# Weight loads issued by GpSimd, its copies and weight arithmetic moved to ScalarE and VectorE

## The chip, the cores and the metric

The kernel runs on one core of a Trainium2 chip. The time is the device time of one execution in microseconds (us); lower is better. The core has TensorE (PE, matmuls and transposes, results into PSUM), VectorE (DVE), ScalarE (ACT), GpSimd (POOL) and SyncE (SP), each with its own queue that it works off in order, and 16 DMA engines that all queues share.

## What is computed

Block-sparse attention over 4 batches, 8 heads, 768 positions in 24 blocks of 32, head size 64 (a block of queries sees its neighbours, the first and the last block and 3 sampled blocks; the first and the last block see all), and then a feed-forward layer (512 to 2048 to 512) with a rational activation on its output, 3072 tokens. Cut to what matters:

```python
def _attn_ref(q, k, v, sampled_blocks):
    scores = scale * np.matmul(q, k.transpose(0, 1, 3, 2))
    ...
    scores = np.where(mask, scores, -1000000000.0)
    attn = np.exp(scores - np.max(scores, axis=-1, keepdims=True))
    attn = attn / (np.sum(attn, axis=-1, keepdims=True) + 1e-09)
    return np.matmul(attn, v).astype(np.float32)

def _moe_ref(x, w_in, w_out, a, b):
    h = x @ w_in
    P = a[0] + a[1] * h + a[2] * h**2 + a[3] * h**3
    Q = 1.0 + np.abs(b[0]) * np.abs(h) + np.abs(b[1]) * h**2
    return ((P / (Q + 1e-06)) @ w_out).astype(np.float32)
```

All inputs arrive as 64-bit numbers (doubles and 64-bit integers). The kernel has to turn them into 32-bit floats itself where they are weights.

## The kernel before

The work is cut into small operations (`Op`), each with the engine or engines that may do it, a price in ns, what it must come after, and a priority (line 116). A planner, `issue` (line 162), goes through them at build time: it always takes the operation that can start first by its prices, ties by priority, and emits it. So the order of every queue is fixed before the run. Where an operation may go to several engines (`among`, line 140; the keys in `ALT = "copsk"` are open to all that are priced, others to the first alone), the planner takes another engine than the home one when the home would start over some 500 ns later (ScalarE 534, GpSimd 243). Operations over 8 priority units ahead of the current feed-forward unit wait. Loads on SyncE are planned on 8 lanes; loads on another queue are not.

*Weights* (`weights`, line 392). `w_in` and `w_out` come as 64-bit words in 16 + 16 pieces of 128 rows x 512 words (512 KB). `one` (line 405) makes for each piece: a load into one of two buffers `wl` (lines 413, 416), issued by SyncE, all in one chain (`behind`); a conversion from the upper words (`convert`, ScalarE, or GpSimd or VectorE); `pack1` to `pack3` on VectorE (lines 425, 428, 431; the last one frees the buffer). A piece of `w_out` is then split into a high part (`out_high`: ScalarE, GpSimd or VectorE) and a low part (`out_low`, line 442: home GpSimd, VectorE allowed). Pieces of `w_in` wait until the four of a group are there; ScalarE takes their largest values (line 375), and after a scale has been worked out (`w_scaled`, line 466) each is scaled (`scaled`, home GpSimd), rounded (`high`, ScalarE) and its rest taken (`low`, line 489, GpSimd).

*Attention* (`attention`, line 688) runs block by block: scores on TensorE (line 761), maxima on VectorE (line 771), exponentials on ScalarE (line 786), transposes on TensorE (line 828) and their eviction by ScalarE (`times`, line 148), values on TensorE (line 863). For batch 0 all keys lie in SBUF (`kall`). Before the scores of a block, GpSimd copies its three sampled key blocks (`copies`, lines 713 to 716; first it loads their numbers into registers, line 667) into one of two buffers `kx`, which the scores of the block two before must have released. Once, GpSimd also copies the first and the last key block (`edges`, line 916), before all `copies`. Later batches read keys by DMA. Values are gathered by DMA on SyncE's queue (lines 839 to 847), queries too (line 639).

*Feed-forward* (`unit`, line 942): 12 chunks of 256 tokens x 8 units. A unit is 24 matmuls (lines 959 to 961), three evaluations of their result on ScalarE (lines 966, 970, 980), and then lines 973 to 1004 on VectorE and two on ScalarE, and 12 matmuls into the output (lines 1015 to 1017). Units of the first two chunks wait for their pieces of the weights. The first units stand between blocks of attention; until the first of them, TensorE fills gaps with dummy matmuls (`fill`, line 160).

Of the kernel before, what the change touches and what calls it, by code (L numbers as in the profile page):

```python
# [11 lines left out]
F32 = mybir.dt.float32  # L12
# [11 lines left out]
def kernel(  # L24
# [367 lines left out]
    def weights():  # L392
# [12 lines left out]
        def one(prio, kind, u, x, before):  # L405
            d = {}
            s_wl = Slot(r_wl)
            s_w = Slot(r_dw) if kind else None

            def load():  # L410
                d["ld"] = early.tile([P, 2 * WC], I32, name="wl", bufs=2)
                if kind:
                    nc.sync.dma_start(out=d["ld"], in_=wo64[x * P:(x + 1) * P])
                    return
                r0 = head(x, 0) * D
                nc.sync.dma_start(out=d["ld"], in_=wi64[r0:r0 + P, u * 2 * WC:(u + 1) * 2 * WC])

            def convert(eng):
                d["w"] = early.tile([P, WC], I32, name="dw", bufs=3) if kind else wi[:, x, u].rearrange("p a n -> p (a n)").bitcast(I32)
                d["words"] = d["ld"].rearrange("p (n w) -> p n w", w=2)  # L420
                times(eng, d["w"].bitcast(F32), d["words"][:, :, 1].bitcast(F32), 2.0 ** -112)

            def pack1():
                w = d["w"]
                nc.vector.tensor_scalar(out=w, in0=w, scalar1=3, scalar2=None, op0=ALU.logical_shift_left)

            def pack2():
                nc.vector.scalar_tensor_tensor(out=d["w"], in0=d["words"][:, :, 0], scalar=29, in1=d["w"], op0=ALU.logical_shift_right, op1=ALU.bitwise_or)

            def pack3():  # L430
                nc.vector.scalar_tensor_tensor(out=d["w"], in0=d["words"][:, :, 1], scalar=-2 ** 31, in1=d["w"], op0=ALU.bitwise_and, op1=ALU.bitwise_or)

            def most():
                if u not in sums:
                    sums[u] = early.tile([P, 8], F32, name="sums")
                bound(d["w"].bitcast(F32), sums[u][:, x:x + 1])

            def out_high(eng):
                times(eng, wo_h[:, x], d["w"].bitcast(F32), 1.0)

            def out_low(eng):
                eng.tensor_tensor(out=wo_l[:, x], in0=d["w"].bitcast(F32), in1=wo_h[:, x].bitcast(F32), op=ALU.subtract)  # L442

            o0 = Op(SY, [(475, 524288)], load, (), prio - 2, takes=[s_wl], behind=before)
            w = [s_w] if kind else []
            o = Op(among("c", SC, sc=520, po=588, ve=335), 0, convert, [o0], prio, takes=w, uses=[s_wl])
            o = Op(VE, 335, pack1, [o], prio, uses=w)
            o = Op(VE, 602, pack2, [o], prio, uses=[s_wl] + w)
            o = Op(VE, 602, pack3, [o], prio, uses=[s_wl] + w)
            if kind:  # L450
                o1 = Op(among("o", SC, sc=520, po=588, ve=335), 0, out_high, [o], prio, uses=w)
                o2 = Op(among("p", PO, po=1225, ve=602), 0, out_low, [o1], prio, uses=w)
                out_ready[x] = [o2]
                decoded.append(o2)
                return o0, o2
            return o0, Op(SC, 613, most, [o], prio)
# [9 lines left out]
    def w_scaled(u, prio, group, sums):  # L466
# [10 lines left out]
        for x in range(NCC):  # L477
            def three(x):
                d, s_ws = {}, Slot(r_dw)

                def scaled(eng):
                    d["w"] = early.tile([P, WC], I32, name="dw", bufs=3).bitcast(F32)
                    times(eng, d["w"], wi[:, x, u].rearrange("p a n -> p (a n)").bitcast(F32), sc[0])

                def high(eng):
                    times(eng, wi[:, x, u, 0], d["w"], 1.0)

                def low(eng):
                    eng.tensor_tensor(out=wi[:, x, u, 1], in0=d["w"], in1=wi[:, x, u, 0], op=ALU.subtract)  # L489

                a = Op(among("s", PO, po=671, ve=396, sc=613), 0, scaled, [o], prio, takes=[s_ws])
                a = Op(among("h", SC, sc=520, po=588, ve=335), 0, high, [a], prio, uses=[s_ws])
                a = Op(among("l", PO, po=1113, ve=602), 0, low, [a], prio, uses=[s_ws])
                in_ready.setdefault(u, []).append(a)
                decoded.append(a)
            three(x)
# [191 lines left out]
    def attention(b, j, prio):  # L688
# [10 lines left out]
        for m, x in enumerate(xs):  # L699
            def one(m, x):  # L700
# [9 lines left out]
                elif near:  # L710
                    s_kx = Slot(r_kx)

                    def copies():
                        rows = sampled_rows(x, mybir.EngineType.Pool)
                        for r in range(NR):
                            nc.gpsimd.tensor_copy(out=kxs[:, s_kx.buf, r].rearrange("p h r -> p (h r)"), in_=kall[:, bass.ds(rows[r], 1)].rearrange("p o h r -> p (o h r)"))

                    a = Op(PO, 1500, copies, [o_setup, chain["edges"]], p - 1, takes=[s_kx], uses=s_kall)
                    deps.append(a)
                    kslots = [s_kx] + s_kall  # L720
                else:
# [443 lines left out]
```

## Time and profile before

| what | value |
|---|---|
| time, median of 3 runs | 870.55 us (868.5, 870.55, 905.55) |
| the profiled execution | 869.87 us |
| its span, first to last instruction | 868.1 us |
| PE busy | 812.3 us (94%) |
| DVE busy | 699.2 us (81%) |
| ACT busy | 578.8 us (67%) |
| POOL busy | 98.7 us (11%) |
| DMA issued through SyncE's queue | 135.27 MB, 60.2% of the 16 engines' span |

The span is what the profile covers; the execution's own time is 1.8 us longer. The busy times are for the whole span; the rows further down give them by stretch. A view by line gives, for a group of like instructions, how many there were, their busy time, the mean duration of one, and how long their engine stood idle just before them and for what. Register loads, branches and DMA issues are not counted as busy. Matmul ends are modelled, so a busy PE is not PE at its peak.

### The profile page before, as it was taken

The page shows a single profiled execution, that of the slowest core. Times are in us where ns is not written, and L with a number is a line of the kernel's source. Part 1 is how long each engine was busy: PE and PEld are TensorE (multiplying, and loading weights), DVE is VectorE, ACT ScalarE, POOL GpSimd, SP SyncE. Part 2 cuts the span into 40 slices and gives each one's busy share as a digit, 9 for nine tenths or more (in the row PEclk, how much of TensorE's full clock was granted, in tenths as well). Part 3 has the DMA queues.
Part 4 walks back from the last instruction along what each step waited for, and adds up shares of the span by engine and source line. Part 5 has one row for each costly group of instructions (what it writes and reads, how often), then busy time and mean ns, then how long its engine had stood idle before and what let it go on. Part 6 is the DMA issues. An engine that isn't in the chain of part 4 may idle for free.

```text
span 868.1 us, 26226 instructions
## 1 busy us (share of the span) xinstructions
PE 812.3 (94%) x10056; PEld 617.4 (71%) x10056; DVE 699.2 (81%) x1773; ACT 578.8 (67%) x1263; POOL 98.7 (11%) x139
## 2 busy tenths in 40 slices
PE   6897757987899999999999999999999999999997
PEld 3555545765677787777777777777777777778885
DVE  2666898999998887778888876877888878887885
ACT  4557477766576676876667677777666676667563
POOL 1332656453200000000000000000000000000000
PEclk9999977999999999999999999999999999999999
DMA  9779668438667866876658667775545646630000
GB/s 218 170 193 237 199 213 217 136 106 219 158 154 178 212 169 169 207 191 175 152 130 201 186 167 174 211 185 163 152 126 153 165 120 171 157 101 23 1 25 25
DMA packets 255916, 136.94 MB, mean 158 GB/s; under 512 B 63408, under 2 KB 245552, under 8 KB 255792
## 3 DMA queue, kind: packets, MB, share of 16 engines
q1 hardware_dynamic: 255792, 135.27, 60.2%
q8 instruction: 80, 1.31, 0.7%
q14 instruction: 44, 0.36, 0.2%
HBM read 124.20 MB, written 11.01 MB: 156 GB/s over the span
## 4 chain that ended last, share of the span: by engine, by line
PE 72%; DVE 12%; DMA 8%; SPq 4%; ACT 2%; issue 2%; ACTq 0%; DVEq 0%
PE acc L1015 9%; PE ph L959 9%; PE acc L1017 9%; PE acc L1016 9%; PE ph L960 8%; PE ph L961 8%; PE av L863 6%; PE m L761 6%; PE m L828 5%; DMA wl<-in_moe_w_out_dram 2%; PE m L522 2%; DMA ld<-in_k_dram 2%; DMA wl<-in_moe_w_in_dram 2%; DMA ld<-in_v_dram 1%; DMA ldq<-in_q_dram 1%
## 5 line engine op out<-in xcount | busy, mean ns | idle before, releaser
L959 PE MATMUL ph<-xh,wi 128*128 128x256 f16 x768 | 210.5, 274 | 1.1 <-DVE tt L976 1.1
L961 PE MATMUL ph<-xh,wi 128*128 128x256 f16 x768 | 209.4, 273 | 1.9 <-POOL wi L489 1.9
L960 PE MATMUL ph<-xl,wi 128*128 128x256 f16 x768 | 209.3, 273 | 0.9 <-DVE xl L908 0.9
L1015 PE MATMUL acc<-wo_h,gh 128*128 128x512 f32 x384 | 162.5, 423 | 0.6 <-ACT ld L148 0.5
L1017 PE MATMUL acc<-wo_h,gl 128*128 128x512 f32 x384 | 153.6, 400 | 7.9 <-DVE gl L1004 7.9
L1016 PE MATMUL acc<-wo_l,gh 128*128 128x512 f32 x384 | 152.7, 398 | 1.2 <-POOL wo_l L442 1.2
L966 ACT ACTIVATE sq<-ph,fc 128x512 f32<-128x512 f32 x96 | 65.9, 686 | 116.1 <-PE ph L961 115.6
L786 ACT ACTIVATE pr<-pr,st 128x256 f32<-128x256 f32 x224 | 111.3, 500 | 33.5 <-DVE st L797 33.4
L959 PEld LDWEIGHTS <-wi 128*128 128x128 f16 x768 | 75.2, 98 | 43.0 <-issue 24.0
L983 DVE SCALAR_TENSOR_TENSOR ab<-sq,absb,ab 128x512 f32<-128x512 f32 x96 | 73.0, 760 | 40.6 <-ACT ab L980 40.4
L771 DVE CUSTOM_DVE_ANT_1 pr<-m,bias 128x256 f32<-128x256 f32 x224 | 85.6, 419 | 12.9 <-PE m L761 12.3
L1017 PEld LDWEIGHTS acc<-wo_h,gl 128*128 128x128 f32 x384 | 72.8, 190 | 27.8 <-DVE gl L1004 10.7
L1015 PEld LDWEIGHTS acc<-wo_h,gh 128*128 128x128 f32 x384 | 73.1, 190 | 20.9 <-issue 6.3
L994 DVE SCALAR_TENSOR_TENSOR gh<-tt,par,rr 128x512 fp32r<-128x512 f32 x96 | 74.0, 771 | 15.8 <-PE acc L1016 8.4
L148 ACT ACTIVATE pT<-m 128x512 f32<-128x512 f32 x112 | 65.9, 594 | 29.3 <-PE m L828 28.7
L961 PEld LDWEIGHTS <-wi 128*128 128x128 f16 x768 | 75.1, 98 | 12.2 <-POOL wi L489 2.5
L1016 PEld LDWEIGHTS acc<-wo_l,gh 128*128 128x128 f32 x384 | 73.0, 190 | 14.5 <-POOL wo_l L442 2.1
L828 PEld LDWEIGHTS m<-ident,pr 128*128 128x128 f32 x448 | 67.8, 206 | 20.8 <-ACT pr L786 7.1
L828 PE MATMUL m<-ident,pr 128*128 128x128 f32 x448 | 75.3, 292 | 7.7 <-ACT pr L786 3.3
L960 PEld LDWEIGHTS <-wi 128*128 128x128 f16 x768 | 75.2, 98 | 7.8 <-issue 0.4
L863 PEld LDWEIGHTS av<-vg,pT 128*32 128x32 f32 x3584 | 55.8, 111 | 28.7 <-issue 13.7
L863 PE MATMUL av<-vg,pT 128*32 128x64 f32 x3584 | 72.4, 224 | 3.7 <-DMA vg<-in_v_dram 2.8
(114 smaller groups left out, 1338.5 us busy)
## 6 DMA issues: line engine op xcount, KB each, us to landing
vg<-in_v_dram SPq DMA_DIRECT2D x312, 64.0 KB, 3.2
vg<-in_v_dram SPq DMA_DIRECT2D x88, 192.0 KB, 3.6
vg<-in_v_dram SPq DMA_DIRECT2D x24, 512.0 KB, 4.6
kall<-ks SPq DMA_DIRECT2D x49, 192.0 KB, 2.8
kall<-ks SPq DMA_DIRECT2D x147, 64.0 KB, 2.1
wl<-in_moe_w_in_dram SPq DMA_DIRECT2D x16, 512.0 KB, 4.5
wl<-in_moe_w_out_dram SPq DMA_DIRECT2D x16, 512.0 KB, 3.9
kall<-ks SPq DMA_DIRECT2D x15, 512.0 KB, 5.2
```

Of the source, the lines that this page charges most:

```text
L771: nc.vector.tensor_tensor_reduce(out=prs[x][:, g].rearrange("p (s r) -> p s r", r=BLK), in0=h["sp"][g], in1=add.rearrange("p (s o) -> p s ...
L786: nc.scalar.activation(out=prs[x][:, g], in_=prs[x][:, g], func=AF.Exp, scale=SCALE, bias=st[:, 6 + g:7 + g], accum_out=st[:, 8 + 2 * m + ...
L828: nc.tensor.transpose(pp[:, jj * P:(jj + 1) * P], pr[:, g, kt:NS * BLK:2], ident)
L863: nc.tensor.matmul(av[rows, g], pT[:, 2 * g + kt, rows], vf[:, head(h4, g), kt * D:(kt + 1) * D], start=(kt == 0 and (n == 1 or (m == 0 an ...
L959: nc.tensor.matmul(o, wh, xh[:, :, cc], start=(cc == 0), stop=False)
L960: nc.tensor.matmul(o, wh, xl[:, :, cc], start=False, stop=False)
L961: nc.tensor.matmul(o, wl, xh[:, :, cc], start=False, stop=(cc == NCC - 1))
L983: nc.vector.scalar_tensor_tensor(out=d["ab"], in0=d["sq"], scalar=absb[:, 1:2], in1=d["ab"], op0=ALU.mult, op1=ALU.add)
L994: nc.vector.scalar_tensor_tensor(out=d["gh"], in0=d["tt"], scalar=par[:, 0:1], in1=d["rr"], op0=ALU.add, op1=ALU.mult)
L1015: nc.tensor.matmul(acc[:, t], ghs, wo_h[:, f], start=(new and e == 0), stop=False)
L1016: nc.tensor.matmul(acc[:, t], ghs, wo_l[:, f], start=False, stop=False)
L1017: nc.tensor.matmul(acc[:, t], gls, wo_h[:, f], start=False, stop=(last and e == 1))
```

## The change

Five things change, all in the first part of the run:

- the loads of weight pieces are issued by GpSimd instead of SyncE (planned at 1000 ns each);
- `convert` and `out_high` may go to ScalarE or VectorE, no longer to GpSimd;
- `out_low` and `low` go to VectorE;
- `scaled` has its home on ScalarE, and may go to VectorE;
- the copies of sampled key blocks, with the register loads before them, go to ScalarE.

GpSimd keeps `edges` and the few operations at the start.

```diff
-                    nc.sync.dma_start(out=d["ld"], in_=wo64[x * P:(x + 1) * P])
+                    nc.gpsimd.dma_start(out=d["ld"], in_=wo64[x * P:(x + 1) * P])
...
-                nc.sync.dma_start(out=d["ld"], in_=wi64[r0:r0 + P, u * 2 * WC:(u + 1) * 2 * WC])
+                nc.gpsimd.dma_start(out=d["ld"], in_=wi64[r0:r0 + P, u * 2 * WC:(u + 1) * 2 * WC])
...
-            def out_low(eng):
-                eng.tensor_tensor(out=wo_l[:, x], in0=d["w"].bitcast(F32), in1=wo_h[:, x].bitcast(F32), op=ALU.subtract)
-
-            o0 = Op(SY, [(475, 524288)], load, (), prio - 2, takes=[s_wl], behind=before)
+            def out_low():
+                nc.vector.tensor_tensor(out=wo_l[:, x], in0=d["w"].bitcast(F32), in1=wo_h[:, x].bitcast(F32), op=ALU.subtract)
+
+            o0 = Op(PO, [(1000, 524288)], load, (), prio - 2, takes=[s_wl], behind=before)
             w = [s_w] if kind else []
-            o = Op(among("c", SC, sc=520, po=588, ve=335), 0, convert, [o0], prio, takes=w, uses=[s_wl])
+            o = Op(among("c", SC, sc=520, ve=335), 0, convert, [o0], prio, takes=w, uses=[s_wl])
...
             if kind:
-                o1 = Op(among("o", SC, sc=520, po=588, ve=335), 0, out_high, [o], prio, uses=w)
-                o2 = Op(among("p", PO, po=1225, ve=602), 0, out_low, [o1], prio, uses=w)
+                o1 = Op(among("o", SC, sc=520, ve=335), 0, out_high, [o], prio, uses=w)
+                o2 = Op(VE, 602, out_low, [o1], prio, uses=w)
...
-                def low(eng):
-                    eng.tensor_tensor(out=wi[:, x, u, 1], in0=d["w"], in1=wi[:, x, u, 0], op=ALU.subtract)
-
-                a = Op(among("s", PO, po=671, ve=396, sc=613), 0, scaled, [o], prio, takes=[s_ws])
+                def low():
+                    nc.vector.tensor_tensor(out=wi[:, x, u, 1], in0=d["w"], in1=wi[:, x, u, 0], op=ALU.subtract)
+
+                a = Op(among("s", SC, sc=613, ve=396), 0, scaled, [o], prio, takes=[s_ws])
                 a = Op(among("h", SC, sc=520, po=588, ve=335), 0, high, [a], prio, uses=[s_ws])
-                a = Op(among("l", PO, po=1113, ve=602), 0, low, [a], prio, uses=[s_ws])
+                a = Op(VE, 602, low, [a], prio, uses=[s_ws])
...
-                        rows = sampled_rows(x, mybir.EngineType.Pool)
+                        rows = sampled_rows(x, mybir.EngineType.Activation)
                         for r in range(NR):
-                            nc.gpsimd.tensor_copy(out=kxs[:, s_kx.buf, r].rearrange("p h r -> p (h r)"), in_=kall[:, bass.ds(rows[r], 1)].rearrange("p o h r -> p (o h r)"))
-
-                    a = Op(PO, 1500, copies, [o_setup, chain["edges"]], p - 1, takes=[s_kx], uses=s_kall)
+                            nc.scalar.activation(out=kxs[:, s_kx.buf, r].rearrange("p h r -> p (h r)"), in_=kall[:, bass.ds(rows[r], 1)].rearrange("p o h r -> p (o h r)"), func=AF.Copy)
+
+                    a = Op(SC, 1100, copies, [o_setup, chain["edges"]], p - 1, takes=[s_kx], uses=s_kall)
```

## Rows read from the trace of the kernel before

**Rows 1.** The windows view: busy time of each engine (and number of instructions) in three stretches of the span, the granted TensorE clock as a share of full speed, the mean busy share of the 16 DMA engines, and GB/s.

```profile
0.00:80.00 80.00, 64.26 (x1013) 40.05 (x1013) 42.53 (x174) 46.80 (x123) 20.52 (x58) 0.96 0.88 209
80.00:240.00 160.00, 126.82 (x1648) 91.00 (x1648) 152.00 (x347) 106.15 (x233) 78.15 (x82) 0.93 0.66 177
240.00:868.10 628.10, 621.25 (x7398) 486.37 (x7396) 504.70 (x1253) 425.82 (x908) 0.00 (x0) 1.00 0.56 146
```

**Rows 2.** The lines view with shapes kept apart, VectorE (DVE), the stretch 0 to 240 us; columns: line, engine, operation, output<-inputs by tile, shapes, count | busy us, mean ns of one | idle before and what ended it.

```profile
L428 DVE SCALAR_TENSOR_TENSOR wi<-wl,wi 128x512 int32<-128x512 int32 x16 | 13.5, 842 | 0.1
L973 DVE TENSOR_TENSOR tt<-tt,sq 128x512 f32<-128x512 f32 x14 | 13.2, 941 | 0.0
L431 DVE SCALAR_TENSOR_TENSOR wi<-wl,wi 128x512 int32<-128x512 int32 x16 | 12.9, 808 | 0.1
L997 DVE SCALAR_TENSOR_TENSOR ab<-ab,gh 128x512 f32<-128x512 f32 x13 | 12.5, 959 | 0.0
L428 DVE SCALAR_TENSOR_TENSOR dw<-wl,dw 128x512 int32<-128x512 int32 x16 | 12.4, 776 | 0.1
L431 DVE SCALAR_TENSOR_TENSOR dw<-wl,dw 128x512 int32<-128x512 int32 x16 | 12.2, 760 | 0.0
L994 DVE SCALAR_TENSOR_TENSOR gh<-tt,par,rr 128x512 fp32r<-128x512 f32 x13 | 12.0, 919 | 0.0
L425 DVE TENSOR_SCALAR dw<-dw 128x512 int32<-128x512 int32 x16 | 11.6, 723 | 4.6 <-ACT dw L148 4.1 <-POOL dw L152 0.5
L983 DVE SCALAR_TENSOR_TENSOR ab<-sq,absb,ab 128x512 f32<-128x512 f32 x14 | 11.5, 821 | 3.7 <-ACT ab L980 3.7
L1000 DVE SCALAR_TENSOR_TENSOR tt<-tt,par,ab 128x512 f32<-128x512 f32 x13 | 11.5, 881 | 0.0
L1004 DVE TENSOR_TENSOR gl<-tt,rr 128x512 fp32r<-128x512 f32 x13 | 10.6, 816 | 0.0
L976 DVE SCALAR_TENSOR_TENSOR tt<-ph,fc,tt 128x512 f32<-128x512 f32 x13 | 9.6, 740 | 0.0
...
L425 DVE TENSOR_SCALAR wi<-wi 128x512 int32<-128x512 int32 x16 | 6.9, 432 | 8.6 <-ACT wi L148 4.9 <-POOL wi L152 3.7
```

**Rows 3.** The same view of VectorE, the stretch 240 to 868 us, in which GpSimd is idle.

```profile
L994 DVE SCALAR_TENSOR_TENSOR gh<-tt,par,rr 128x512 fp32r<-128x512 f32 x83 | 62.1, 748 | 15.8 <-PE acc L1016 8.4 <-ACT sq L966 4.4 <-PE acc L1017 2.6
...
L976 DVE SCALAR_TENSOR_TENSOR tt<-ph,fc,tt 128x512 f32<-128x512 f32 x83 | 61.9, 745 | 0.4
...
L1004 DVE TENSOR_TENSOR gl<-tt,rr 128x512 fp32r<-128x512 f32 x84 | 57.7, 687 | 2.0
L997 DVE SCALAR_TENSOR_TENSOR ab<-ab,gh 128x512 f32<-128x512 f32 x83 | 56.9, 685 | 0.0
```

**Rows 4.** The lines view of GpSimd (POOL), the whole span.

```profile
L716 POOL COPY kx<-kall 128x128 f32 x66 | 24.2, 404 | 37.8 <-PE m L761 34.3 <-issue 1.6 <-POOL kx L716 1.0
L442 POOL TENSOR_TENSOR wo_l<-dw,wo_h 128x512 fp32r<-128x512 f32 x16 | 23.3, 1458 | 20.5 <-ACT wo_h L148 20.0
L489 POOL TENSOR_TENSOR wi<-dw,wi 128x512 f16<-128x512 f32 x16 | 22.0, 1385 | 8.1 <-ACT wi L148 8.1
L152 POOL TENSOR_SCALAR dw<-wi,scw 128x512 f32<-128x512 f32 x13 | 11.6, 898 | 7.9 <-DVE scw L353 7.7
L152 POOL TENSOR_SCALAR wo_h<-dw 128x512 fp32r<-128x512 f32 x7 | 6.9, 984 | 19.6 <-DVE dw L431 14.0 <-DVE st L808 3.0 <-DVE st L811 2.7
L152 POOL TENSOR_SCALAR dw<-wl 128x512 f32<-128x512 f32 x6 | 5.3, 875 | 5.7 <-DMA wl<-in_moe_w_out_dram 5.7
L152 POOL TENSOR_SCALAR wi<-wl 128x512 f32<-128x512 f32 x6 | 4.4, 739 | 18.9 <-DMA wl<-in_moe_w_in_dram 18.9
```

**Rows 5.** The lines view with shapes kept apart, ScalarE (ACT), 0 to 240 us.

```profile
L786 ACT ACTIVATE pr<-pr,st 128x256 f32<-128x256 f32 x62 | 30.8, 499 | 12.9 <-DVE st L797 12.9
...
L148 ACT ACTIVATE wi<-wl 128x512 f32<-128x512 f32 x10 | 6.7, 673 | 11.1 <-DMA wl<-in_moe_w_in_dram 11.1
...
L148 ACT ACTIVATE wo_h<-dw 128x512 fp32r<-128x512 f32 x9 | 5.7, 630 | 9.2 <-DVE dw L431 9.2
...
L148 ACT ACTIVATE dw<-wi,scw 128x512 f32<-128x512 f32 x3 | 2.2, 719 | 0.9 <-POOL wi L489 0.9
...
L298 ACT ACTIVATE absb<-par 128x2 f32<-128x2 f32 x1 | 0.2, 203 | 3.4 <-DMA par<-in_moe_b_dram 3.4
```

**Rows 6.** The source view of line 667, the loads of a sampled block's number into a register: queue, operation, count: duration in ns as min/median/max, first and last start in us.

```profile
L667 POOLq TENSOR_LOAD <-ix x22: 726/730/2653, 17.2 to 170.5; - x22
```

**Rows 7.** The timeline of SyncE's queue: start us, duration us, line, transfer, how many in a row. The first three loads of weights.

```profile
13.33 0.43 SPq L416 DMA_DIRECT2D wl<-in_moe_w_in_dram  x1
...
29.32 1.85 SPq L416 DMA_DIRECT2D wl<-in_moe_w_in_dram  x2
```

**Rows 8.** The waits view of SyncE's queue, 0 to 240 us: who waited for whom, us in total, times, longest.

```profile
SPq L413 <- DVE dw L431: 17.5, 6, 7.3
```

**Rows 9.** The waits view of TensorE (PE), 0 to 240 us.

```profile
PE acc L1017 <- DVE gl L1004: 7.1, 5, 3.1
...
PE m L761 <- ACT kt L148: 3.3, 1, 3.3
PE m L828 <- ACT pr L786: 3.3, 3, 2.1
...
PE av L863 <- DMA vg<-in_v_dram: 2.8, 3, 1.5
```

## What the change is predicted to do

> **What bounds the kernel now.** Read the windows view first. After 240 us TensorE is busy 621.25 of 628.10 us at the full clock and GpSimd does nothing [rows 1]; nothing that the change touches runs there. So all of it must show in the first 240 us, where TensorE has 191.1 busy us, some of it dummy matmuls of line 160, and 49 idle. In 80 to 240 us VectorE is busy 152.00 of 160 us (95%), ScalarE 106.15 (66%), GpSimd 78.15: there VectorE sets the pace, and TensorE waits for its last step of a unit (7.1 us) more than for any single thing [rows 1, 9]. In 0 to 80 us no compute engine is full (VectorE 42.53, ScalarE 46.80), but the DMA engines are busy 0.88 of the time [rows 1].
>
> Then the lines view of VectorE, before and after 240 us, is to be laid side by side. The same instruction on the same tile is longer while GpSimd works: line 973 takes 941 ns early, line 997 takes 959 against 685 later; line 976, which reads one of its tensors from PSUM, takes 740 early and 745 late [rows 2, 3]. So GpSimd's work stretches VectorE's instructions that take two tensors from SBUF.
>
> **Part 1: GpSimd's compute goes away, VectorE is not stretched any more.** Working with the late durations as the undisturbed ones (748 for lines 994, 983, 1000; 687 for 973 and 1004; 685 for 997 and for 428 and 431, of the same form) [rows 2, 3]: line 973 14 x 254, 997 13 x 274, 994 13 x 171, 983 14 x 73, 1000 13 x 133, 1004 13 x 129 ns = 13.7 us; 428 and 431 16 x (157 + 123 + 91 + 75) = 7.1 us; 425 on the dw tile 16 x (723 - 432) = 4.7 us. Together 25.5 us of VectorE. [...]
>
> **Part 2: the low parts move to VectorE.** 16 of line 442 (1458 ns) and 16 of line 489 (1385 ns) leave GpSimd [rows 4]. On VectorE the nearest row is 687 ns, a tensor_tensor of 128x512 from SBUF [rows 3]: 32 x 0.687 = 22.0 us. Parts 1 and 2 together: -3.5 us of VectorE, counted in full since VectorE is 95% busy where most of it falls. Bounds: -25.5 (the new work all fits into VectorE's idle time before 80 us) to +22 (the stretch stays).
>
> **Part 3: shorter chain.** A group of four low parts in a row takes 4 x 1.385 = 5.5 us on GpSimd and 4 x 0.687 = 2.7 us on VectorE [rows 3, 4]: 2.8 us for each of four groups of w_in, 11 us if each were waited for. VectorE has other work meanwhile, so I take -4; bounds 0 and -11.
>
> **Part 4: loads leave SyncE's order.** The first weight load is issued at 13.33 us, the next two only at 29.32, although there are two buffers [rows 7]: they stood behind other loads. From GpSimd, which has nothing else in line, the first two can go at once and each later one when its buffer is free. VectorE has 80 - 42.5 = 37.5 idle us before 80 us [rows 1]; a piece decoded there instead of later takes 0.432 + 3 x 0.687 = 2.5 us off the full stretch (lines 425, 428, 431, low) [rows 2, 3]. The DMA engines have 0.12 x 80 = 9.6 us left there, and 512 KB at 209 GB/s are 2.5 us [rows 1], so three to four pieces: I take three, -7.5 us; bounds 0 and -19 (half of the idle 37.5; the other half I put on the start, when nothing has landed).
> SyncE stood 17.5 us in 6 waits for a weight buffer [rows 8], with gathers of values queued behind. That stall goes to GpSimd's queue, where only the next weight load and one copy (edges) wait behind it. On TensorE the relief is worth little: it waits 2.8 us for values in all [rows 9]. I count 0 (bounds 0 and -2.8).
> On the other side, a second load of 512 KB goes out beside the first k, v and q loads: 2.5 us at the same rate, and edges now stands in a queue of loads that wait for buffers, with the key copies behind it. I take +2, bounds 0 and +5.
>
> **Part 5: ScalarE gets the rest.** 66 key copies of 128x128: the nearest rows are 203 ns (2 columns) and 499 ns (256 columns with an exponential) [rows 5]; I take the middle, 0.35: 23.1 us. With them go 22 register loads of 0.730 us [rows 6], 16.1 us in ScalarE's queue, half hidden behind the instruction in progress: 8. Six conversions onto wi and six onto dw, 12 x 0.673 = 8.1; 13 scalings x 0.719 = 9.3; 7 high parts x 0.630 = 4.4 [rows 4, 5]. Sum 53 us. If they fall as GpSimd's work did (78.15 of 98.67 us after 80 us), ScalarE has 106 + 42 = 148 of 160 us to do in the full stretch, 12 us of idle time instead of 54 [rows 1]. It fits, so the floor is 0. The planner may give convert, high part of w_out and scaling to VectorE when ScalarE would start over 500 ns later. TensorE now waits 6.6 us for ScalarE in the two rows shown [rows 9]; with a quarter of the idle time left such waits could grow fourfold, +20. I take +6, nearer the floor because of that choice.
>
> **Part 6: do loads from GpSimd stretch VectorE?** No row shows one. The 130 GpSimd operations of [rows 4] cost 25.5 us, 0.2 us each; 32 loads at that rate cost 6.3 us, the other bound is 0. I take +1, since a load reads no tile of SBUF.
>
> **Sum:** -3.5 - 4 - 7.5 + 2 + 6 + 1 = -6.0. The profiled execution took 869.87 us (span 868.1, 1.8 around it), 0.7 below the median of 870.55: 869.87 - 6.0 = 863.9, so **864 us**, 0.75% under the median.
>
> **Rivals.**
> *ScalarE becomes the bound (slower).* GpSimd stood idle 18.9 + 5.7 us until a weight load landed and 34.3 us until TensorE had released a key buffer [rows 4]; that hurt nobody, since its queue was short. In ScalarE's order the same wait holds every exponential and eviction behind it. All of the first and half of the second is 42 us, against 12 us of idle time left: the other 30 take the place of the +6: 864 - 6 + 30 = 888. It decides from the point where ScalarE's waits in 80 to 240 us exceed those 12 us. Against it: its order is planned, so a wait comes only where the plan errs, and two engines may convert.
> *Decoding moves wholly forward (faster).* If the loads run ahead, VectorE fills half of its idle 37.5 us before 80 us: -19 instead of -7.5, and ScalarE, relieved later on, costs 0: 864 - 11.5 - 6 = 846. For it: the buffers stood empty early [rows 7]. Against: DMA engines at 0.88 there.
> *The loads go no earlier.* The transfers are bound by the DMA engines, not by who issues; parts 3 and 4 give nothing but the +2: -3.5 + 2 + 6 + 1 = +5.5, 875. For it speak the same 0.88 and TensorE's small DMA wait. [...]
> [...]
>
> **How the numbers follow.** Forecast (853 to 873) 0.30; decoding wholly forward 0.26; ScalarE the bound 0.20; loads no earlier 0.16; loads held up 0.08. Two per cent, 17.4 us, is about what a measurement of this kernel can tell from no change: faster means under 853, slower over 888. Faster: most of the 846 case and a little of the forecast, 0.27. Slower: over half of the 888 case, and the tails of 875 and 878, 0.19. Within 2%: 0.54. For 8 in 10 the range must hold 846 and nearly reach the 888 case's middle: 843 to 889.
>
> **What would show it.** In the changed profile: GpSimd's busy time near nothing; lines 973, 994, 997, 1000 and 1004 before 240 us at their late durations (part 1; if still stretched, part 6); the low parts at about 0.69 us (part 2); the second and third weight loads long before 29 us, and VectorE busier before 80 us (part 4); a first score no later than before, or the +2 is too small; ScalarE's busy time in 80 to 240 us near 148 us and TensorE's waits for it near 13 us (part 5). The forecast fails if ScalarE's waits for weight loads or key buffers grow past some 12 us, or if TensorE is full well before 240 us, which would be the faster case.

## The result: a little slower, and most of the loss where nothing was changed

| | before | after |
|---|---|---|
| time, median | 870.04 us (6 runs, from 868.5) | 876.7 us (6 runs, 875.38 to 879.64) |
| span of the profiled execution | 868.1 us | 875.3 us |

The ratio is 1.0089, 95% interval 1.0065 to 1.0114: 6.7 us slower, where 864 us had been forecast. One disturbed run of the kernel before (905.55) is left out of the ratio.

The windows view of the kernel after, in the stretches of [rows 1]:

```profile
0.00:80.00 80.00, 62.24 (x776) 37.29 (x777) 45.91 (x170) 47.76 (x132) 8.01 (x20) 0.91 0.93 216
80.00:240.00 160.00, 138.55 (x1915) 99.59 (x1914) 143.30 (x398) 127.33 (x310) 11.31 (x21) 0.90 0.66 173
240.00:875.30 635.30, 625.56 (x7396) 488.07 (x7395) 505.56 (x1251) 425.88 (x910) 0.00 (x0) 1.00 0.56 145
```

GpSimd is nearly empty (19.3 us in all), VectorE has 8.7 us less to do in 80 to 240 us, ScalarE 21.2 more. The surprise is the last line: the stretch after 240 us holds nearly the same work and grew from 628.1 to 635.3 us.

The lines view of VectorE, 0 to 240 us, against [rows 2 and 3]:

```profile
L442 DVE TENSOR_TENSOR wo_l<-dw,wo_h 128x512 fp32r<-128x512 f32 x16 | 11.0, 687 | 2.1 <-ACT wo_h L148 2.0
...
L489 DVE TENSOR_TENSOR wi<-dw,wi 128x512 f16<-128x512 f32 x16 | 10.5, 687 | 1.1 <-ACT wi L148 1.0
...
L994 DVE SCALAR_TENSOR_TENSOR gh<-tt,par,rr 128x512 fp32r<-128x512 f32 x13 | 9.6, 746 | 0.0
L973 DVE TENSOR_TENSOR tt<-tt,sq 128x512 f32<-128x512 f32 x14 | 9.6, 686 | 0.0
...
L997 DVE SCALAR_TENSOR_TENSOR ab<-ab,gh 128x512 f32<-128x512 f32 x13 | 8.9, 684 | 0.0
...
L425 DVE TENSOR_SCALAR dw<-dw 128x512 int32<-128x512 int32 x16 | 6.7, 420 | 1.1 <-ACT dw L148 1.1
```

The stretch is gone: lines 973, 994 and 997 (941, 919 and 959 ns before) are within 2 ns of their late durations in [rows 2 and 3] or of the row taken for them, line 425 on dw took 723 and takes 420, and the low parts take the 687 ns that were forecast. ScalarE, 0 to 240 us, against [rows 5]:

```profile
L716 ACT ACTIVATE kx<-kall 128x128 f32 x66 | 15.6, 304 | 8.7 <-PE m L761 7.2 <-issue 0.8 <-DVE mx L620 0.4
...
L148 ACT ACTIVATE dw<-wl 128x512 f32<-128x512 f32 x14 | 9.6, 683 | 5.4 <-DMA wl<-in_moe_w_out_dram 5.4
...
L148 ACT ACTIVATE wi<-wl 128x512 f32<-128x512 f32 x11 | 7.4, 670 | 5.3 <-DMA wl<-in_moe_w_in_dram 5.3
```

A key copy takes 304 ns, and ScalarE now waits 7.2 us for TensorE before the copies. For weight loads it waits 5.4 + 5.3 us; in the kernel before these two waits were 6.0 and 11.1 us [rows 5 for the second]. The start, as the timelines of GpSimd and of SyncE's queue show it:

```profile
1.30 1.20 POOL L416 DMA_DIRECT2D wl<-in_moe_w_in_dram  x2 [0.35 <-issue]
...
17.90 0.55 POOL L416 DMA_DIRECT2D wl<-in_moe_w_in_dram  x1 [14.90 <-DVE wi L431]
```

```profile
3.41 7.17 SPq L542 DMA_DIRECT2D ab<-in_k_dram  x2
```

Two weight loads leave at 1.30 us instead of 13.33 [rows 7]. But SyncE's next two loads of k now take 7.17 us to issue. The same line of the kernel before:

```profile
3.24 2.79 SPq L542 DMA_DIRECT2D ab<-in_k_dram  x2
```

The DMA view has the two loads of k ahead of them landing after 9.2 us (median) instead of 4.6, and the first score stands at 25.3 us instead of 20.8.

**Where after 240 us?** In the two traces VectorE and ScalarE run the same instructions in the same order from 249 us of the kernel before on. So the start of one instruction tells how far one kernel lies behind the other. The last step of one unit (line 1004), before and then after:

```profile
337.09 0.69 DVE L1004 TENSOR_TENSOR gl<-tt,rr 128x512 fp32r<-128x512 f32 x1
```

```profile
338.29 0.69 DVE L1004 TENSOR_TENSOR gl<-tt,rr 128x512 fp32r<-128x512 f32 x1
```

Here the changed kernel is 1.2 us behind, at the end of the span 7.2 us (875.3 against 868.1). So 6.0 of the 7.2 us are lost behind this instruction. Windows of 30 us find two gaps in TensorE, at the last loads of v of batches 2 and 3. After, then before:

```profile
360.00:390.00 30.00, 28.44 (x363) 21.38 (x361) 22.25 (x62) 21.07 (x48) 0.00 (x0) 1.00 0.76 194
...
545.00:575.00 30.00, 27.73 (x333) 20.52 (x332) 19.75 (x55) 18.84 (x43) 0.00 (x0) 0.94 0.73 183
```

```profile
360.00:390.00 30.00, 29.75 (x395) 23.58 (x394) 23.10 (x67) 22.32 (x53) 0.00 (x0) 1.00 0.74 195
...
545.00:575.00 30.00, 30.00 (x389) 23.73 (x390) 22.59 (x63) 21.39 (x51) 0.00 (x0) 1.00 0.82 211
```

TensorE is busy 3.6 us less in the two windows together; the rest of the 6.0 us is not accounted for. In the second gap the granted clock falls as well (0.94). ScalarE's timeline at the first gap, after and then before; the bracket is its wait for a load of v (issued at line 604), whose largest values line 375 takes:

```profile
362.44 0.62 ACT L990 ACTIVATE rr<-rr 128x512 f32<-128x512 f32 x1
367.08 0.63 ACT L375 ACTIVATE scrap<-ld 128x512 f16<-128x512 f32 x1 [4.03 <-DMA ld<-in_v_dram]
...
368.19 0.50 ACT L786 ACTIVATE pr<-pr,st 128x256 f32<-128x256 f32 x1
```

```profile
361.16 0.61 ACT L990 ACTIVATE rr<-rr 128x512 f32<-128x512 f32 x1
363.28 0.63 ACT L375 ACTIVATE scrap<-ld 128x512 f16<-128x512 f32 x1 [1.51 <-DMA ld<-in_v_dram]
```

Line 990, ahead of the scan, starts 1.3 us later than before, the scan itself 3.8 us later: ScalarE stands 4.03 us ahead of it instead of 1.51. Behind the scan stand the exponentials (line 786) that TensorE needs. After 240 us TensorE waits for them in the changed kernel; the kernel before has no such wait:

```profile
PE m L828 <- ACT pr L786: 2.6, 3, 1.1
```

The load was issued at 362.61 (before: 360.34), so load to scan is 4.5 us instead of 2.9. At the second gap, the last load of v to its scan takes 5.0 us (556.08 to 561.04) instead of 3.5 (551.79 to 555.29). On the DMA engines a packet of another queue differs. The DMA view of 361 to 368 us after:

```profile
q8 instruction: 1, 0.02, 1.3%
...
ld<-in_v_dram SPq DMA_DIRECT2D x1, 256.0 KB, 4.5
```

Before, 359 to 364 us has no packet on that queue, and the same load lands after 2.9 us:

```profile
ld<-in_v_dram SPq DMA_DIRECT2D x1, 256.0 KB, 2.9
```

The landing of a load is told by sixteen updates of a semaphore (14000 for the 875 transfers of a run), as many as the page counts DMA engines. For these two loads of the changed kernel fifteen come within 3.19 and 3.23 us of the issue, the last at 4.46 and 4.87 us. In the kernel before the last two come at 2.89 and 2.92 us, and at 3.22 and 3.42. So fifteen of the sixteen updates were there in time.

Queue q8, "instruction" on the page, has 80 packets of 16 KB in a run, each 0.9 to 1.9 us long. They follow TensorE's stream: from the first to the last of them 20154 of its instructions start in the kernel before and 20082 in the kernel after, waits among them, which is 255 and 254 to a packet, and e13 below, with a longer stream, has 81. So they are taken here as fetches of TensorE's instructions. In the changed kernel two of them start at 364.02 and 558.35 us, while those two loads are under way; in the kernel before at 364.44 (after the scan) and 555.10 us, 3.3 us after the load was issued. Not every such meeting costs time: in the kernel before the load of v issued at 353.37 us meets a fetch at 356.75, its last update comes 1.6 us behind the others, and ScalarE waits 1.56 us for it, yet TensorE is busy 60.00 us from 300 to 360 us and 29.75 of the next 30. The changed kernel has 156 dummy matmuls instead of 128, 62 instructions more with their waits, and the fetches fall elsewhere on the later work. Whether that costs time is what the first experiments ask. It does: the traces below put some 6 us on two fetches.

### The profile page after: what moved, and what is told of

Read it like the earlier page. It is cut to its first block, busy times and chain, and to the rows that moved or that the text cites. A ratio compares the mean times of both kernels' runs of the same rounds, so it can differ in the third digit from the quotient of the medians.

```text
span 875.3 us, 26253 instructions
## 1 busy us (share of the span) xinstructions
PE 826.4 (94%) x10084; PEld 625.0 (71%) x10084; DVE 694.8 (79%) x1816; ACT 601.0 (69%) x1350; POOL 19.3 (2%) x41
## 4 chain that ended last, share of the span: by engine, by line
PE 72%; DVE 4%; ACT 3%; DMA 3%; SPq 1%; issue 1%; ACTq 0%; DVEq 0%; POOLq 0%
PE ph L959 10%; PE acc L1015 9%; PE acc L1017 9%; PE acc L1016 9%; PE ph L960 8%; PE ph L961 8%; PE m L761 6%; PE av L863 6%; PE m L828 5%; PE m L522 1%; DMA wl<-in_moe_w_in_dram 1%; DMA ld<-in_v_dram 1%; PE m L897 1%; DMA wl<-in_moe_w_out_dram 1%; ACT sq L966 0%
## 5 line engine op out<-in xcount | busy, mean ns | idle before, releaser
L1015 PE MATMUL acc<-wo_h,gh 128*128 128x512 f32 x384 | 164.6, 429 | 0.1
L828 PE MATMUL m<-ident,pr 128*128 128x128 f32 x448 | 77.9, 297 | 13.9 <-ACT pr L786 9.1
L994 DVE SCALAR_TENSOR_TENSOR gh<-tt,par,rr 128x512 fp32r<-128x512 f32 x96 | 71.7, 747 | 15.4 <-PE acc L1016 8.4
L863 PEld LDWEIGHTS av<-vg,pT 128*32 128x32 f32 x3584 | 57.7, 114 | 25.6 <-issue 11.8
L863 PE MATMUL av<-vg,pT 128*32 128x64 f32 x3584 | 74.6, 229 | 1.1 <-ACT pT L148 1.1
```

The source lines that it names most:

```text
L828: nc.tensor.transpose(pp[:, jj * P:(jj + 1) * P], pr[:, g, kt:NS * BLK:2], ident)
L863: nc.tensor.matmul(av[rows, g], pT[:, 2 * g + kt, rows], vf[:, head(h4, g), kt * D:(kt + 1) * D], start=(kt == 0 and (n == 1 or (m == 0 an ...
L994: nc.vector.scalar_tensor_tensor(out=d["gh"], in0=d["tt"], scalar=par[:, 0:1], in1=d["rr"], op0=ALU.add, op1=ALU.mult)
L1015: nc.tensor.matmul(acc[:, t], ghs, wo_h[:, f], start=(new and e == 0), stop=False)
```

## The experiments

All medians stand beside runs of the kernel before on the same chip (868.6 to 869.6 us). "Old length" means that dummy matmuls were left out or doubled until TensorE's stream was as long as in the kernel before. The edits shift line numbers by up to 3.

### Is it the length of the stream? (e1, e2)

```diff
 # e1, changed kernel; e2, kernel before: "for _ in range(2 if len(calls) <= 31 else 1):"
+        calls.append(0)
+        if len(calls) > 31:
             nc.tensor.matmul(fills[0][:, 0]...)
```

> The changed kernel without the first 31 of its dummy matmuls (62 instructions on TensorE, so that its instruction stream is as long as that of the kernel before). Nothing else differs. Theory A (the stretch after 240 us): both kernels have the same order there, and about 5.5 of the 6.7 us are lost in two places, 362 to 370 and 555 to 565 us, where a fetch of TensorE's instructions (16 KB on one DMA engine) falls on a load of v for which ScalarE's scan waits; with the stream of the old length the fetches fall elsewhere, and the time goes to 870 to 872 us. Theory B (the first 240 us): the weight loads that run ahead of the first k and q loads cost the time; the length of the stream does nothing, and the time stays at 875 to 878 us.

> The kernel before with the first 31 dummy matmuls issued twice, so that TensorE's instruction stream is as long as that of the changed kernel; they fall into the first 20 us, where TensorE waits for loads. Theory A: the loss appears without the change, 874 to 877 us, at the same places of the order. Theory B: no change, 869 to 872 us.

Measured: e1 868.04 us (under the expected 870 to 872), ratio 1.0013 (0.9985 to 1.0041); e2 876.16 us, ratio 1.007 (1.0042 to 1.0098). The changed kernel without 31 dummies shows no sure cost; the kernel before with 31 more loses about as much as the change did. In e1 TensorE is busy 30.00 and 29.96 of 30 us in the two windows. In the trace of e2 only the second load is late: at the first place the fetch starts 2.48 us after the load is issued, and the load lands after 3.1 us.

### Is it ScalarE's wait for v? (e5, e6)

The planner is told that the loads of v in batches 2 and 3 land 1.8 us later, so it places other work before the scan. Streams and TensorE's order stay.

```diff
-                end = dma + 900
+                end = dma + 900 + o.allow
...
+                o.allow = 1800 if b > 1 else 0
                 los.append(Op(SC, 613, most, [o], prio, uses=[slot]))
```

> The changed kernel; the planner allows 1.8 us more for the landing of the loads of v of batches 2 and 3, on which ScalarE's scan of largest values (line 375) waits. So only the scans stand later in ScalarE's order (and a few operations after them on ScalarE and VectorE); the orders of TensorE, SyncE and GpSimd, the number of dummy matmuls and with them the length of TensorE's instruction stream are those of the changed kernel. Theory (an instruction fetch of TensorE delays a load of v by some 1.5 us, ScalarE stands at the scan meanwhile and its exponentials come late): the fetches still fall on those loads, but ScalarE has other work first; its waits for ld on line 375 near 362-372 and 555-562 us fall from 4.0 and 4.1 us to under 1.5 in all, TensorE's busy time in 360-390 and 545-575 us is above 29.3 of 30, and the median is 870 to 872.5 us. Rival (the longer stream costs TensorE its time directly, by its own fetches, or in another way that does not go through ScalarE's wait): 875 to 878 us, and the same two gaps in TensorE.

> The same edit on the kernel before, whose loads of v meet no fetch at those places. Theory: nothing to win but a part of the 2.2 us that ScalarE waits there anyway; the median is 867.5 to 870.5 us. Rival (the allowance helps of itself, by a better order on ScalarE, whatever the fetches do): 862 to 866 us, as much won as in the run before this one.

Measured: e5 869.57 us (just under the expected 870 to 872.5), ratio 1.0023 (0.9999 to 1.0047), by the ratios 5.7 us less than the changed kernel (1.0089 - 1.0023); e6 867.83 us, 0.9994 (0.9971 to 1.0016), no sure gain. In e5 a fetch still starts behind each load (load 360.42, fetch 362.58; 551.98 and 553.67). It makes only the second load late (fifteen updates by 3.26 us, the last at 4.36); the first lands after 2.98 us, so the first place does not test the wait. ScalarE's wait on line 375 is gone from both places, and TensorE is busy 29.36 and 29.94 of 30 us:

```profile
360.00:390.00 30.00, 29.36 (x389) 23.42 (x389) 23.85 (x68) 22.58 (x52) 0.00 (x0) 1.00 0.83 199
...
545.00:575.00 30.00, 29.94 (x362) 23.85 (x361) 23.32 (x63) 22.11 (x49) 0.00 (x0) 1.00 0.91 224
```

The stream is as long as in the changed kernel and a load is late, but from line 1004 (336.04 us) to the end e5 loses nothing against the kernel before. So at the second place the loss goes through that wait and not through TensorE's own fetching.

### Is it where the fetches fall? (e13 to e15)

A longer stream as such, or the time of the dummies, would still fit e1 and e2. Small dummies (32 columns instead of 512, two instructions each) lengthen the stream; 256 instructions more are about one packet, by the 255 and 254 above.

```diff
+        calls.append(0)
+        if len(calls) <= 97:   # e13, changed kernel; before: 128 in e14, 31 in e15
+            nc.tensor.matmul(fills[0][:, 0, 0:32], ident16, ident16[:, 0:32], start=True, stop=True)
```

> The changed kernel; each of its first 97 dummy matmuls is followed by a small one (32 columns instead of 512), two instructions each. TensorE's stream is then 194 instructions longer than that of the changed kernel and 256 longer than that of e1_after_31_fewer. One packet of the instruction queue holds 256 instructions of TensorE, so from there on the fetches fall on the same work as in e1. Theory (it is where the fetches fall that costs, not how long the stream is): 867 to 871 us, ScalarE's waits for ld at line 375 near 2 us in each of the two places instead of 4.0 and 4.1, TensorE's busy time there 29.8 of 30 us. Rival (each instruction more costs its share): at least the 876.7 us of the changed kernel, by its own rate of 6.7 us for 62 some 20 us more.

> The kernel before; each of its 128 dummy matmuls is followed by a small one: 256 instructions more, one whole packet, so that the fetches fall after them where they fell. Theory: 868 to 870.5 us. Rival (length): 62 more cost 7 us in e2_before_31_more, so 256 cost some 28: 890 us and more.

> The kernel before; its first 31 dummy matmuls are followed by small ones: 62 instructions more, as in e2_before_31_more, but next to no time of TensorE (31 times 32 columns instead of 31 times 512). Theory: the fetches fall as in e2, 874 to 877 us, TensorE's busy time in 545 to 575 us near 28 of 30. Rival (in e2 it was the time of the 31 dummies themselves that cost): 868 to 870 us.

Measured: e13 868.23 us, ratio 0.9991 (0.997 to 1.0012); e14 871.2 us, 1.0024 (1.001 to 1.0038); e15 873.06 us, 1.0056 (1.0028 to 1.0083). With 194 instructions *more* the changed kernel is 8.5 us faster; with 256 more the kernel before loses 2 us by its ratio (its median is 0.7 us above the expected range), not 28; with 62 more it loses 5 (873.06 us, just under the expected 874 to 877) and gets both gaps. In the first 80 us TensorE is busy 63.54 us in e13, with 93 matmuls more than the kernel after, which has 62.24 us. The windows of e13, then of e15:

```profile
360.00:390.00 30.00, 29.99 (x408) 23.43 (x407) 23.26 (x67) 21.80 (x51) 0.00 (x0) 1.00 0.77 198
545.00:575.00 30.00, 29.91 (x395) 23.51 (x393) 23.41 (x66) 21.20 (x47) 0.00 (x0) 1.00 0.79 204
```

```profile
360.00:390.00 30.00, 28.53 (x341) 21.41 (x340) 21.06 (x60) 19.78 (x47) 0.00 (x0) 0.94 0.68 180
545.00:575.00 30.00, 27.95 (x364) 21.42 (x354) 21.04 (x58) 19.36 (x44) 0.00 (x0) 1.00 0.77 196
```

The two places in seven traces (before, after, e1, e2, e13 to e15) give 14 pairs of a load of v and the fetch next to it. In five the fetch starts 1.4 to 2.3 us after the load is issued, and load to scan is 4.5 to 5.0 us (both of after and of e15, one of e2); in nine it starts 2.5 us after it or later, and load to scan is 2.9 to 3.7. Eight further pairs in e3, e4, e7 and e8 are like the nine (3.0 us or later, 3.0 to 3.7). The start of the fetch alone is no sharp border: at the first place of e5 it starts 2.16 us after the load, and the load is not late.

The start of line 1004 and the end of the span, both against the kernel before, tell what the late part costs in each profiled execution (a minus is ahead):

| kernel | late loads | behind at line 1004, us | behind at the end, us | lost between, us |
|---|---|---|---|---|
| after | 2 | 1.2 | 7.2 | 6.0 |
| e15 | 2 | -3.4 | 2.4 | 5.8 |
| e2 | 1 | 1.4 | 4.3 | 2.9 |
| e5 | 1, scan placed later | -1.1 | -1.1 | 0.0 |
| e1 | 0 | -3.1 | -4.3 | -1.2 |
| e13 | 0 | 1.8 | 1.3 | -0.5 |
| e14 | 0 | 2.3 | 2.9 | 0.6 |

Each late load costs about 3 us where the scan stands in the way. The first part of single executions scatters by several us, and what e14 loses in its profiled execution is lost there, not at the two places.

The queue's line counts the extra packet in e13 (80 packets in the kernel after):

```profile
q8 instruction: 81, 1.33, 0.7%
```

The rival "length" falls (e13, e14), and so does "time of the dummies" (e15). How a fetch holds the last update of a load up is not shown; that it is the fetch rests on where it falls in these runs.

### What the loads are worth (e3, e4, e7)

```diff
 # e3, changed kernel, old length: the first weight load waits for edges
-            o0 = Op(PO, [(1000, 524288)], load, (), prio - 2, ...)
+            o0 = Op(PO, [(1000, 524288)], load, () if before else (chain["edges"],), prio - 2, ...)
 # e4, changed kernel, old length: loads back on SyncE
-                    nc.gpsimd.dma_start(out=d["ld"], in_=wo64[x * P:(x + 1) * P])
+                    nc.sync.dma_start(out=d["ld"], in_=wo64[x * P:(x + 1) * P])
...
-            o0 = Op(PO, [(1000, 524288)], load, (), prio - 2, ...)
+            o0 = Op(SY, [(475, 524288)], load, (), prio - 2, ...)
 # e7, kernel before, old length: the loads alone on GpSimd, planned at 1000 ns there
```

> The changed kernel, its first weight load placed behind the copy of the first and last key block in GpSimd's queue (about 18 us), and 45 dummy matmuls left out so that TensorE's stream has the old length. Theory A for the late part and B for the early one together: the first score is back at about 21 us (25.3 in the changed kernel), and the time is 2 to 5 us under that of the run with 31 fewer dummies. If the early lag is made good anyway before 240 us, it equals that run within 1 us. Theory B alone: 870 or less, whatever the late part.

> The changed kernel with its weight loads issued by SyncE as before (40 dummies left out, stream of the old length): only the copies and the weight arithmetic are moved. My prediction's part 4 had 5.5 us of gain from the moved loads: then this is 5 us slower than the run with 31 fewer dummies. Theory B (the loads in front of k and q are the harm): 3 to 5 us faster than that run, 866 to 869.

> The kernel before with the weight loads alone moved to GpSimd (the first 14 dummy matmuls stand twice, so that TensorE's stream has the old length). The prediction gave this part -7.5 + 2 = -5.5 us. From e4_compute_only (the changed kernel with the loads on SyncE, 869.3 us) against e1_after_31_fewer (868.0 us) the loads alone are worth about -1: 866 to 870 us, the first score some 3 to 5 us later than in the kernel before and the lag made good by 240 us. Rival (without the other parts, GpSimd's own work stands in one queue with the loads, so low parts and key copies wait behind a load that waits for its buffer): 873 to 880 us.

Measured: e3 870.79 us, 1.0031 (1.0011 to 1.0051); e4 869.29 us, 0.9998 (0.9979 to 1.0017); e7 866.31 us, 0.998 (0.9955 to 1.0004). Holding the loads back brings the first score from 25.8 (e1) only to 23.8 us, not to 21, and wins no time: e3 is 2.7 us slower than e1 by the medians, 1.6 by the ratios, which is neither of the expected cases and not sure. So nothing is seen of the lag at the start by the end; e1, with the late first score, is 3.1 us ahead of the kernel before at line 1004. What the loads are worth is near nothing: by the ratios -1.7 us alone (e7), +1.3 on top of all the rest (e1 against e4; by the medians -1.3), and neither is sure. e4 is thus neither 5 us slower nor 3 to 5 us faster than e1.

### What the rest is worth (e8 to e12)

```diff
 # e8 and e9: changed kernel with the key copies on GpSimd as before; e9 to e12 with the allowance of e5, all old length
-                            nc.scalar.activation(out=kxs[:, s_kx.buf, r]..., func=AF.Copy)
+                            nc.gpsimd.tensor_copy(out=kxs[:, s_kx.buf, r]...)
...
-                    a = Op(SC, 1100, copies, ...)
+                    a = Op(PO, 1500, copies, ...)
 # e10: the whole change; e11: the whole change with three key buffers
-    r_kx = Ring(range(2))
+    r_kx = Ring(range(3))
 # e12: as e9, loads on SyncE
```

> The changed kernel with the copies of sampled key blocks (and the register loads before them) back on GpSimd (the first 19 dummy matmuls left out, so that TensorE's stream has the old length). Theory, that ScalarE's copies cost little because VectorE sets the pace in 80 to 240 us: 867 to 872 us, ScalarE some 15 to 20 us less busy in 80 to 240 us. Where the copies on ScalarE were the price of the change: 862 to 866 us. Where GpSimd's copies wait in its queue behind loads that wait for a buffer: 873 to 880 us, with TensorE waiting for kx at the scores.

> The kernel of e8_copies_on_gpsimd (everything changed but the key copies, TensorE's stream of the old length) with the allowance of e5_after_allowance. If the copies on ScalarE are the price of the change: 861 to 864 us, 4 to 6 us under the next run. If the 862.9 of e8, a median of four, was luck (its profiled span and that of e1_after_31_fewer reach 240 us within half a microsecond of each other): 866 to 868 us, within 1.5 us of the next run. It is also the version that is to beat both kernels.

> The changed kernel with the allowance and without its first 31 dummy matmuls, so that it differs from e9 only in the key copies, which ScalarE makes. From e1_after_31_fewer (868.0) and what the allowance gave the kernel before (0.8): 867 to 868.5 us.

> The kernel of e10 with three buffers of key copies instead of two (and edges copied into all three; 26 dummy matmuls fewer, so that the stream has the same length). The copies stay on ScalarE, and so does their busy time of some 20 us; what changes is how long ScalarE stands in order until the scores of the block two before have released a buffer (7.2 us in the changed kernel). If that wait is the price of the copies: 862 to 865 us and waits of ScalarE for scores at the copies under 2 us. If the work itself and its register loads are the price: within 1.5 us of e10. If both cost nothing: e9, e10 and this one lie within 1.5 us of each other.

> The changed kernel with key copies back on GpSimd and loads back on SyncE, so that only the weight arithmetic is moved (to VectorE and ScalarE), with the allowance and the old length of the stream. Against e6_before_allowance (867.8) it prices parts 1 to 3 of the prediction and the arithmetic's share of part 5, against e9 the loads. If the parts add up (loads alone gave -2.3, loads and arithmetic together -5.7): 864 to 866 us. If the arithmetic only pays where loads run ahead: 867 to 869 us.

| kernel (stream of the old length) | median, us | ratio to before |
|---|---|---|
| e6: before, allowance | 867.83 | 0.9994 (0.9971 to 1.0016) |
| e12: arithmetic moved, allowance | 866.48 | 0.9973 (0.9954 to 0.9991) |
| e9: arithmetic and loads, allowance | 863.95 | 0.9941 (0.9915 to 0.9967) |
| e10: and copies: the whole change, allowance | 866.33 | 0.9979 (0.9958 to 1.0001) |
| e11: the same, three key buffers | 871.17 | 1.0033 (1.0014 to 1.0052) |
| e8: arithmetic and loads, no allowance | 862.88 (4 runs) | 0.9912 (0.9878 to 0.9945) |

Step by step, by the ratios: arithmetic -1.8 us (e6 to e12), loads -2.8 (e12 to e9), copies +3.3 (e9 to e10), together -1.3. Each ratio is known to about 0.2% (1.9 us) on either side, so of the three steps only that of the copies is clear of the noise, and just so. The one contrast without allowance, e8 to e1, gives 8.8 us for the copies, from four runs of e8. e9 and e8 beat the kernel before by 0.6 and 0.9%, and the changed one by more; their intervals overlap, so the allowance adds nothing sure to a stream of the old length. The copies are a price of the change, as e8 was to tell, but e9 lies only 2.4 us under e10, between the two cases that were expected. e10 lies just under its expected 867 to 868.5 us, e12 between its two cases. ScalarE was 5 us less busy in e8 than in e1 in 80 to 240 us (125.3 against 130.3), not 15 to 20. GpSimd's queue held neither e7 nor e8 up. Each step is small against the scatter of single executions: the profiled spans of e9 (865.9) and e10 (863.2) stand the other way round.

e11 refutes my reason for that price. Its wait for key buffers is gone, as the waits of ScalarE in e10 and then e11 show (0 to 240 us), and it is 4.8 us slower than e10:

```profile
ACT kx L719 <- PE m L764: 7.5, 3, 6.8
```

```profile
ACT kx L719 <- PE m L764: 1.6, 3, 1.0
```

In its profile the granted clock is 0.87 and 0.88 up to 80 and 240 us (0.96 and 0.93 in e10), and TensorE waits 10.4 us for gathered values. The third buffer gives the planner another order; which part of it costs was not tried.

GpSimd's copies in e8 cost VectorE next to nothing. The copies, and line 973 of the kernel before (975 here) beside them:

```profile
L718 POOL COPY kx<-kall 128x128 f32 x66 | 22.8, 384 | 41.6 <-PE m L763 37.2 <-issue 2.1 <-PE m L830 1.2
```

```profile
L975 DVE TENSOR_TENSOR tt<-tt,sq 128x512 f32<-128x512 f32 x14 | 9.7, 694 | 0.0
```

694 ns beside 22.8 us of GpSimd's copies, 686 without them, 941 before.

## Why the prediction was wrong

**The step that failed** is in its first paragraph: "nothing that the change touches runs there. So all of it must show in the first 240 us". What runs after 240 us was indeed not touched, but when TensorE's instructions arrive was. The plan of the changed kernel filled more gaps with dummies, the stream grew by 62 instructions, and two fetches fell on loads of v that stood at the head of ScalarE's order. That is worth 5.7 to 8.5 us by the ratios against 1.0089 (5.7 in e5, 6.6 in e1, 8.5 in e13, each known to some 3 us), and 6.0 us in the profiled execution. No term and no rival of the prediction had it, and it turned a change worth about nothing into a loss. The measured 876.7 us lies inside the forecast's range of 843 to 889 us and between the 875 and 878 us of two other cases, "loads no earlier" and "loads held up"; that is luck: in the runs the loads did go earlier, and none was seen held up by VectorE.

**Part 1** was right in cause and size: VectorE's instructions fell to the durations of [rows 3], and they follow GpSimd's arithmetic: line 973 takes 685 ns in e12, where it is gone, and 852 in e7, where it stays. One thing was wrong in it: the stretch was put on all 130 GpSimd operations. The 66 copies do not cause it (e8); which of the others do was not tried, and how they stretch VectorE's instructions was not shown.

**Part 2** was right: 687 ns, 32 of them, 21.5 us. VectorE's busy time before 240 us fell from 194.5 to 189.2 us, -5.3 against -3.5.

**Parts 1 to 3 together** were to give -7.5 us, and with the arithmetic's share of part 5 some -5. e12 gave -1.8. The step "counted in full since VectorE is 95% busy" was too large: VectorE's busy time in 80 to 240 us fell from 151.6 (e6) to 143.3 us (e12), and little of that came out at the end. What limits that stretch instead was not isolated.

**Part 4** had -7.5 + 2 = -5.5 us; e7 gives -1.7, e12 to e9 -2.8, e4 to e1 +1.3. The loads did leave earlier (1.30 us), but slowed the loads of k beside them (7.17 instead of 2.79 us of issuing; 7.18 in e7, the loads alone, and 2.82 in e3, where they are held back). VectorE decoded nine pieces before 80 us instead of seven, where three more had been taken, so what fails is mainly what an earlier piece is worth. The rival "decoding moves wholly forward" falls with VectorE's busy time before 80 us: it rose by 3.4 us (42.53 to 45.91), not by half of the idle 37.5. The +2 was too small for the first score (4.5 us later), of which no cost is seen in the end (e3). The rival "loads go no earlier" (+5.5) falls with its premise, since they did go earlier; that its gain of nothing from the loads is close to what was measured is luck. That the transfers are bound by the DMA engines fits the loads of k, which landed after 9.2 us instead of 4.6 with two weight loads issued ahead of them.

**Part 5** was mis-sized in its work: 53 us were estimated for ScalarE, its busy time before 240 us rose by 22.1 us (from 152.95 to 175.1). The copies cost 304 ns, not 350; register loads are not in the busy time; and VectorE took seven conversions, two scalings and two high parts. ScalarE stood at 127 of 160 us, not 148, and its waits there for weight loads and key buffers were 10.9 us of 32.7 idle, so the rival "ScalarE becomes the bound" is refuted as it was put. TensorE's waits for ScalarE in the two rows that were used came to 6.9 us instead of 6.6, not to 13. The +6 had some 3.5 for the copies by their share of the 53 us, and e9 to e10 gives 3.3; with work of less than half the size and the wait for key buffers refuted (e11), that agreement is luck, and what the copies cost by stays open.

**Part 6**: no residual stretch is seen. The 878 us of "loads held up" stand on a delay of GpSimd's loads by VectorE that no run shows: issuing a load took 530 ns on GpSimd (median; 755 at most), with VectorE busy 143.30 of the 160 us from 80 to 240 us. Landings are 1.2 to 1.3 us later than from SyncE (5.7 against 4.5 us, 5.2 against 3.9).

With fetches that hit nothing the change is worth between -1.3 and +1.1 us (e10 against e6; e13 -0.8; e1 +1.1), where -6.0 was forecast: the gains of parts 1 to 4 came to under half of their size (-1.8 and -2.8 us, where some -10.5 had been summed, with the arithmetic's share of part 5), and the copies of part 5 took most of them back. The rest, up to the +7.7 us of the measured ratio, is the fetch.

## What to carry to other kernels

An edit at the start of a kernel can cost time at its end without changing anything there (here 6.0 of 7.2 us): it shifted where TensorE's instructions are fetched. Before explaining a change of under one per cent, run the kernel once more with the number of its dummy instructions altered, and compare stretches whose order did not change. What made the shift expensive is an instruction that already waited for its load (ScalarE 1.51 us in the kernel before, 4.03 after), standing in order before work that TensorE needs; a planner that allows 1.8 us more for such a load took that wait out of the way in e5.

## What was not expected of the hardware

- With a single 16 KB packet (1.49 and 0.88 us long in the kernel after) the last of sixteen updates of a 256 KB load that was under way came 1.0 to 1.6 us after the other fifteen (load to scan 4.5 to 5.0 us against 2.9 to 3.7). One such delay with the waits behind it cost 2.9 us (e2), two cost 5.8 and 6.0 (e15, after).
- The loss does not grow with the stream's length: 62 instructions more cost the kernel before 5 to 6 us by the ratios (e15, e2), 256 more cost 2 (e14), 194 more gave the changed kernel 8.5 us back (e13).
- GpSimd's copies of 128x128 (e8) leave line 973 on VectorE at 694 ns, where GpSimd's former mix of work had brought the same line to 941.
